# GLA recurrence and squared-ReLU layers on one Trainium2 core: fixed engine orders, two load queues, a finer first unit

## The chip, the cores and the metric

The kernel runs on one core of one Trainium2 chip. A core has a matrix engine (TensorE: PE, and PEld for its weight loads), VectorE (DVE), ScalarE (ACT), GpSimd (POOL) and SyncE (SP), each of which works through its own list of instructions in order, and 16 DMA engines. Here SP and POOL issue the DMAs: SP's on a queue that the profile calls q1 hardware_dynamic, POOL's on q0 software_dynamic. The metric is the device time of one execution in microseconds.

## The reference

```python
for t in range(S):                       # q, k, v, alpha: [4, 8, 768, 48], alpha in 0.8 to 1.0
    state = alpha[:, :, t, :, None] * state + einsum('bhd,bhe->bhde', k[:, :, t], v[:, :, t])
    y[:, :, t] = einsum('bhd,bhde->bhe', q[:, :, t], state)
x = y.transpose(0, 2, 1, 3).reshape(3072, 384)
out = square(maximum(x @ w_in, 0)) @ w_out      # w_in [384, 2048], w_out [2048, 384], all float32
```

A gated linear recurrence for 4 batches of 8 heads over 768 steps, and behind it two dense layers with a squared ReLU between them.

## The kernel before

**Units.** The 768 steps of a batch are cut in 3 stretches of T = 256 tokens; with 4 batches that makes G = 12 units, ordered stretch by stretch, so that units 0 to 3 are the first stretch of each batch. Two neighbouring tokens share a partition. Inside a unit the recurrence is computed as attention in two chunks: cumulated logarithms of alpha give decay factors, which multiply k and q; keys against queries give scores, a causal mask is laid over them, and scores times v plus queries times the carried state give x.

**Names.** Each operation has a name with its unit g, and the prediction uses them:

- `lda`, `ldk`, `ldq`, `ldv` load a unit's alpha, k, q, v (line 526; 1024 runs of 384 bytes, 384 KB), into one of 4 buffers;
- `ln` and `lm` take logarithms of alpha (lines 542, 604, 636, 675; from unit 2 on behind `pr`, a product of neighbours, line 633), `m1`, `m1i`, `m1s` sum them on TensorE (lines 548, 608, 642), `ei`, `ea`, `es`, `ec` are exponentials of the sums (563, 565, 621, 623, 653 and on), `bk`, `aq`, `lb` derive the other token's factors;
- `ekm` and `eqm` multiply k and q by the factors (578, 704, 709), `tr` transposes both (on TensorE for units 0 to 2, lines 590 and 732, with `et` bringing them back from PSUM, 597 and 739; by DMA on SP from unit 3 on, line 720), `vc` casts v (572, 699, 700);
- `p0` (and `p1` in unit 0) are the scores (898), `mk0` and `mk1` mask them (909), `kv` with `sa`, `sc`, `sd` forms the state (769, 864 to 875), `y` is the output of the attention (790, 801, 830, 837);
- `xe` takes x out of PSUM (929), `xt` transposes it (on TensorE, line 944, for units 0 to 3, by DMA on SP, line 950, from unit 4 on), `xv` brings it back (956, 958);
- `s1_g_u`, u = 0 to 7, is the first dense layer, 6 matmuls each (line 1000); `re` the ReLU out of PSUM (1008 on ScalarE, 1010 on VectorE), from two PSUM banks used by turns; `sq` the square (1018 VectorE, 1021 POOL, 1022 ScalarE); `s2_g_j_sg` the second layer, 4 matmuls each (1040); `oe` takes the result out (1047, 1049) and `out` stores it (1056).

In unit 0 the front works by halves of the heads, with an x = 0 or 1 in the name (`ln0_0`, `ln1_0`).

**What sets the order.** Every operation is entered with its reads and writes (`Program.add`, line 72). `Program.schedule` (line 117) plays the program through with a cost for each operation, priorities with hand-set offsets (`MOVED`, `CHOSEN`) and a model of the DMA queues; out of it come the engine of each operation and the order on each engine. `place` then puts the semaphore waits in, and each engine runs its list in order, so that a waiting instruction holds all behind it. `fill` (line 229) puts matmuls on zeros into TensorE's list wherever it would be idle before the first dense matmul; 34 of them here (line 1094).

**Loads and weights.** Units 1 and 2 load on POOL's queue, all others, the DMA transposes and all stores on SP's. The weights come in WS = 2 pieces each, cast to bfloat16 by the DMA, on POOL's queue. Loads are gated on the landing of others, and from unit 5 on on work of the unit before:

```python
AFTER = {1: (0, "a"), ("win", 0): (0, "k"), ("win", 1): (0, "k"), 2: ("win", 0), ("wout", 0): ("win", 1),
         ("wout", 1): (2, "k"), 3: ("wout", 0)}
AFTER.update({g: (g - 1, "q") for g in range(4, G)})
BEHIND = {"a": "ln", "k": "ekm", "q": "tr0_", "v": "tr0_"}     # of unit g - 1, for g >= 5
```

**The table load.** ScalarE's first operation, `table` (line 439), loads the set of function tables that has both logarithm and exponential. Nothing depends on it by name; its priority puts it first.

## Time and profile before

| what | value |
|---|---|
| timed runs | 175.56, 178.09, 178.64 us, median 178.09 |
| profiled execution, span | 178.0 us |
| PE busy | 168.6 us, 95% |
| DVE, ACT, POOL busy | 120.3, 119.4, 24.2 us |
| first dense matmul (L1000) | 18.21 us |
| HBM read, written | 25.17 MB, 4.72 MB |

The profiled execution is a run of its own; its time is its span, first to last instruction, 178.0 us. A line of a timeline gives start, length, engine, source line, operation, output and inputs, the count of merged instructions, and in brackets how long the engine had been idle before and what ended that. A line of a table of groups gives busy time and mean ns of one, then the idle time ahead of it. The matmuls' ends are modelled.

### The profile page before, as it was taken

Reading aid. Unit: us, or ns where it says so; the run is one execution under the profiler, and the core shown is the slowest. Engines: PE = TensorE matmul, PEld = TensorE weight load, DVE = VectorE, ACT = ScalarE, POOL = GpSimd, SP = SyncE. Lnnn points to the kernel's source line nnn. Section 1 sums busy time; section 2 is a strip of 40 time slices with the busy share of each in tenths; the row PEclk is TensorE's granted clock in tenths of the full one; section 3 lists DMA queues with packets and bytes.
Section 4 is the critical chain, followed back from the end, with each engine's and each line's share of the span. In section 5 each row is a group of like instructions: output and inputs, shape, how many; then the busy total and the mean of one; then the engine's idle time right before and its main releaser. Section 6 shows DMA issues by size and latency. Waiting matters only on the chain.

```text
span 178.0 us, 5087 instructions
## 1 busy us (share of the span) xinstructions
PE 168.6 (95%) x2232; PEld 130.6 (73%) x2234; DVE 120.3 (68%) x194; ACT 119.4 (67%) x214; POOL 24.2 (14%) x32
## 2 busy tenths in 40 slices
PE   7998998999996999999779999999999999999994
PEld 2655787856875778787558878878778787788773
DVE  5478579789885679984838876967958835423230
ACT  3838787867828588696388759859579554566450
POOL 3920951020304224200000000000000000000000
DMA  5999999979999799998999897999999692040022
GB/s 142 344 283 204 250 271 219 243 188 232 295 218 170 206 228 127 280 216 137 290 210 165 203 242 176 243 176 206 251 215 181 146 186 41 0 133 4 0 88 88
DMA packets 71030, 33.36 MB, mean 187 GB/s; under 512 B 67552, under 2 KB 67808, under 8 KB 71008
## 3 DMA queue, kind: packets, MB, share of 16 engines
q1 hardware_dynamic: 69024, 26.75, 67.6%
q0 software_dynamic: 1984, 6.29, 14.9%
q8 instruction: 17, 0.28, 0.6%
q14 instruction: 5, 0.04, 0.1%
HBM read 25.17 MB, written 4.72 MB: 168 GB/s over the span
## 4 chain that ended last, share of the span: by engine, by line
PE 74%; DMA 15%; ACT 5%; POOL 2%; DVE 1%; issue 1%; SPq 1%
PE psWH L1000 32%; PE psO L1040 29%; DMA raw<-in_v_dram 10%; DMA raw<-in_alpha_dram 5%; PE psZ L769 2%; PE psX L801 2%; POOL raw L526 2%; PE psX L898 2%; PE psX L790 2%; PE psX L970 1%; ACT rr L1008 1%; PE psZ L898 1%; PE psWH L642 1%; ACT vbf L700 1%; PE psZ L732 1%
## 5 line engine op out<-in xcount | busy, mean ns | idle before, releaser
L1000 PE MATMUL psWH<-xt,win 128*128 128x256 bf16 x576 | 73.9, 275 | 2.9 <-ACT rr L1008 1.8
L1000 PEld LDWEIGHTS psWH<-xt,win 128*128 128x128 bf16 x576 | 65.3, 145 | 8.1 <-ACT rr L1008 2.5
L1040 PE MATMUL psO<-wout,gt 128*128 128x384 bf16 x368 | 68.9, 326 | 1.9 <-ACT osb L1047 1.9
L1008 ACT ACTIVATE rr<-psWH 128x512 bf16<-128x512 f32 x85 | 50.1, 595 | 20.3 <-PE psWH L1000 18.6
L1040 PEld LDWEIGHTS psO<-wout,gt 128*128 128x128 bf16 x368 | 34.7, 98 | 20.5 <-ACT osb L1047 2.2
L1018 DVE TENSOR_TENSOR gt<-rr 128x1024 bf16<-128x1024 bf16 (+1 forms) x39 | 24.1, 622 | 25.3 <-ACT rr L1008 25.2
L909 DVE TENSOR_TENSOR pm<-psZ,caus 128x1024 bf16<-128x1024 f32 x12 | 14.6, 1219 | 2.4 <-PE psZ L898 2.4
L1022 ACT ACTIVATE gt<-rr 128x1024 bf16<-128x1024 bf16 (+1 forms) x18 | 15.2, 843 | 0.4
L909 DVE TENSOR_TENSOR pm<-psX,caus 128x1024 bf16<-128x1024 f32 x12 | 14.6, 1219 | 1.1 <-PE psZ L898 1.1
L929 ACT ACTIVATE xbf<-psX 128x768 bf16<-128x768 f32 x11 | 8.9, 809 | 7.1 <-PE psX L790 6.4
L700 ACT ACTIVATE vbf<-raw 128x768 bf16<-128x768 f32 x9 | 7.6, 841 | 8.6 <-DMA raw<-in_v_dram 8.6
L1047 ACT ACTIVATE osb<-psO 128x384 f32<-128x384 f32 x17 | 8.3, 489 | 5.2 <-PE psO L1040 4.8
L704 DVE TENSOR_TENSOR qks<-raw,eq 128x384 bf16<-128x384 f32 x18 | 9.8, 575 | 2.5 <-DMA raw<-in_q_dram 2.3
L1094 PE MATMUL psO<-zero 128*128 128x512 bf16 (+1 forms) x32 | 9.9, 437 | 1.5 <-DVE zero L447 1.3
L709 DVE TENSOR_TENSOR qks<-raw,ek 128x768 bf16<-128x768 f32 x11 | 10.5, 952 | 0.5 <-ACT ek L621 0.4
L1010 DVE TENSOR_SCALAR rr<-psWH 128x512 bf16<-128x512 f32 x11 | 7.6, 689 | 1.7 <-PE psWH L1000 1.2
L662 DVE TENSOR_TENSOR ek<-ek,raw 128x384 f32<-128x384 f32 x9 | 6.3, 705 | 1.4 <-ACT ek L653 1.4
L864 DVE TENSOR_TENSOR smd<-psZ,sbd 128x384 bf16<-128x384 f32 x8 | 4.4, 556 | 3.9 <-PE psX L790 3.9
L635 POOL TENSOR_TENSOR prd<-raw 128x384 f32<-128x384 f32 x4 | 4.0, 1002 | 19.5 <-DMA raw<-in_alpha_dram 19.5
L1094 PEld LDWEIGHTS psO<-zero 128*128 128x128 bf16 x34 | 3.2, 110 | 4.5 <-issue 1.9
L675 ACT ACTIVATE la<-raw 128x384 f32<-128x384 f32 x8 | 4.1, 518 | 3.4 <-DMA raw<-in_alpha_dram 3.2
L636 ACT ACTIVATE lab<-prd 128x384 bf16<-128x384 f32 x10 | 5.2, 521 | 1.7 <-DVE prd L633 1.7
(118 smaller groups left out, 171.7 us busy)
## 6 DMA issues: line engine op xcount, KB each, us to landing
out_dram<-osb SPq DMA_DIRECT2D x11, 384.0 KB, 4.1
raw<-in_alpha_dram SPq DMA_DIRECT2D x10, 384.0 KB, 3.6
raw<-in_k_dram SPq DMA_DIRECT2D x10, 384.0 KB, 5.3
raw<-in_q_dram SPq DMA_DIRECT2D x10, 384.0 KB, 3.9
raw<-in_v_dram SPq DMA_DIRECT2D x10, 384.0 KB, 5.2
win<-in_moe_w_in_dram POOLq DMA_DIRECT2D x2, 768.0 KB, 10.9
wout<-in_moe_w_out_dram POOLq DMA_DIRECT2D x2, 768.0 KB, 9.0
raw<-in_alpha_dram POOLq DMA_DIRECT2D x2, 384.0 KB, 4.6
```

The source lines that it names most:

```text
L700: name=f"vc{g}", alts={"act": (lambda e: e.activation(vout, vin, AF.Copy), act_ns(2 * HD))})
L704: add("dve", lambda e, j=j, dst=dst: e.tensor_tensor(dst, RAW[r][:, 2, :, j, :].rearrange("p (n x) d -> p n x d", x=2), EQ[la][:, j].rearr ...
L709: add("dve", lambda e, a=a, E=E: e.tensor_tensor(QKS[qs][:, a, :, :, 0:D], RAW[r][:, 1 + a].rearrange("p h j d -> p j h d"), E[la][:].rear ...
L909: add("dve", lambda e, hf=hf, psT=psT: e.tensor_tensor(PM[pm][:, hf].rearrange("p r n j t -> p (r n) (j t)"), psT[:, :, :].rearrange("p r ...
L929: add("act", lambda e: e.activation(XBF[x2][:], psX[:, :, 0:HD], AF.Copy), act_ns(2 * HD), p0 + 6100, reads=[("ps", "X", 0), ("ps", "X", 1 ...
L1000: ins = pe.matmul(psH[hb][:, i * T:(i + 1) * T], WIN[:, kk, hidden(fj)], mov, start=(kk == 0), stop=(kk == KT - 1))
L1008: add("act", lambda e, hb=hb, rr=rr: e.activation(rr, psH[hb], AF.Relu), act_ns(512), pu + 600, reads=[("ps", "H", hb)], writes=[("rr", rb ...
L1018: add("dve", lambda e, dst=dst, sq=sq: e.tensor_tensor(dst, sq, sq, ALU.mult), 148 + k * 267, pu + 1200, reads=[("rr", rb, h) for h in ran ...
L1022: "act": (lambda e, dst=dst, sq=sq: e.activation(dst, sq, AF.Square), act_ns(k * 512))})
L1040: ins = pe.matmul(psS, GT[gt][:, fj, j, :], WOUT[:, fj, :], start=(fj == 0), stop=(fj == FT - 1))
L1047: add("act", lambda e, j=j, psS=psS: e.activation(OSB[ob][:, j], psS, AF.Copy), act_ns(DM), ps_ + 700, reads=[keyS], writes=[("osb", ob, j ...
L1094: pr.fill(lambda n: lambda pe: pe.matmul(psO[:, 0:n], ZERO[:, 0:128], ZERO[:, 0:n], skip_group_check=True), ((512, 216, 420), (256, 109, 2 ...
```

## The change

It replaces the scheduler by five written-out lists, one for each engine, which name each operation once; an operation's engine is the list in which it stands. The fillers have a notation of their own in these lists ("~"), which the lists don't use. `place` and `emit` stay. Beside it:

- Loads from unit 1 on and stores may stand in SP's or POOL's list. Of the 49 load operations 29 stand in POOL's, and 6 of the stores. The gates on other loads go, but for two (alpha of unit 1 behind alpha of unit 0, the first piece of w_in behind k of unit 0), and so do those on the unit before.
- Unit 0's alpha is loaded in two halves; its state product is split in two steps (`kva0`, `kvb0`), its x is taken out, transposed and brought back in two halves (`xe0_0`, `xe1_0` and so on), and its second half's transposes use other PSUM banks.
- Each weight is loaded in three pieces, a quarter, a quarter and a half.
- ScalarE's `table` stands behind `xv0_0`, VectorE's fill of the zeros that the fillers used in the middle of its list.
- 55 ReLUs are ScalarE's and 41 VectorE's, and 20, 21 and 19 of the squares ScalarE's, VectorE's and POOL's.

```diff
-    HOP = 35
...
-    MOVED = {
...
-    CHOSEN = {
...
+    HALVED = {"qks": 3, "kqt": 3, "raw": 3, "ek": 3, "eq": 3, "acm": 2, "laf": 2, "xbf": 2, "xt": 2}
...
-    def schedule(self):
...
+    def schedule(self, tables, filler):
+
+        named = {o.name: o for o in self.ops}
+        queues = {}
+        for e, text in tables.items():
+            queues[e] = []
+            for word in text.split():
+                if word[0] == "~":
+                    after, n = filler[0], int(word[1:])
+                    o = Op({"pe": (filler[1](n), 0)}, 0, "fill")
+                    o.idx = len(self.ops)
+                    o.deps = {after: True}
+                    self.ops.append(o)
                 else:
...
+                    o = named.pop(word)
+                o.eng = e
+                o.fn, o.cost = o.alts[e]
+                o.pos = len(queues[e])
+                queues[e].append(o)
+        assert not named, sorted(named)
+        for o in self.ops:
+            if o.sem is not None:
+                key = o.sem[0] + o.eng
+                if key not in self.dma_sems:
+                    self.dma_sems[key] = self.nc.alloc_semaphore("d_" + key)
+                self.dma_count[key] = self.dma_count.get(key, 0) + 1
+                o.sem = (key, self.dma_count[key])
+        self.order = queues
+        at = dict.fromkeys(queues, 0)
+        free = dict.fromkeys(queues, 0)
+        left = len(self.ops)
+        while left:
+            before = left
+            for e, q in queues.items():
+                while at[e] < len(q) and all(d.end is not None for d in q[at[e]].deps):
+                    o = q[at[e]]
+                    o.start = max([free[e]] + [d.end for d in o.deps])
+                    free[e] = o.end = o.start + 1
+                    at[e] += 1
+                    left -= 1
+            assert left < before, [q[at[e]].name for e, q in queues.items() if at[e] < len(q)]
...
+TABLES = {
+    "pe": """
+        m10_0 tr00_0 m11_0 tr10_0 tr01_0 tr11_0 kva0 p1_0 p0_0 m11 y0 tr1_1 kvb0 xt1_0 xt0_0 tr0_1 s1_0_0 p0_1 m1i2
+        s1_0_1 kv1 s1_0_2 s1_0_3 y1 s1_0_4 s1_0_5 m1s2 xt1 s1_0_6 s1_0_7 tr0_2 s1_1_0 s1_1_1 m1i3 s1_1_2 s2_0_0_0
+        s1_1_3 s1_1_4 s2_0_0_1 tr1_2 s1_1_5 s1_1_6 m1s3 p0_2 s2_0_0_2 s2_0_0_3 s1_1_7 s2_0_1_0 s2_0_1_1 kv2 s2_0_1_2
...
+    "act": """
+        ln0_0 ei0_0 ea0_0 ln1_0 et00_0 ei1_0 ec0_0 ea1_0 ec1_0 et10_0 et11_0 et01_0 ln1 copycaus ei1 ea1 ec1 xe0_0
+        ln2 xv0_0 table ei2 re0_0 re0_1 sq0_1 ea2 re0_2 ec2 xe1 re0_4 re0_5 re0_6 re0_7 ln3 es2 et0_2 re1_1 ei3
+        re1_2 ea3 re1_4 sq0_7 ec3 re1_6 es3 oe0_0 vc2 sq1_6 vc3 oe0_1 xe2 ln4 ei4 ea4 re2_0 ec4 lm4 re2_3 es4 sq2_1
...
+    "dve": """
+        zlab0 zlinc zident zones zlstr zown zcaus1 zqks0 own0 own1 zcaus zlaf0 ekm0_0 eqm0_0 ekm1_0 eqm1_0 zlaf1
+        zqks1 mk1_0 mk0_0 sa0 eqm1 ekm1 xe1_0 zlab1 et1_1 xv1_0 et0_1 sc0 mk1_1 bk2 mk0_1 sa1 zqks2 re0_3 sq0_3 ekm2
+        xv1 sq0_5 re1_0 sc1 eqm2 re1_3 bk3 sq1_3 et1_2 sq1_1 re1_5 mk1_2 mk0_2 ekm3 sa2 sc2 pr4 sd2 eqm1_3 re1_7
+        eqm0_3 xv2 sa3 sc3 oe1_0 re2_1 eqm1_4 ekm4 re2_2 lb4 mk0_3 mk1_3 sq2_3 re2_5 eqm0_4 sa4 re2_6 pr7 sc4 xv3
+        lb5 eqm1_5 bk5 oe2_0 eqm0_5 re3_2 ekm5 mk0_4 mk1_4 re3_4 sq3_5 lb6 sa5 re3_7 sc5 ekm6 re3_6 zzero mk0_5
...
+    "pool": """
+        scaus1 sident slinc slstr lda1 ldq1 lda2 ldk1 scaus vc0 win0 win1 win2 pr2 ldk2 wout0 ldq2 vc1 wout1 wout2
+        sd0 ldv2 ldk3 pr3 aq2 sd1 sq0_6 aq3 sq1_5 ldq4 ldk4 sq1_7 sd3 bk4 ldq5 lda7 lda6 out0_1 vc4 ldv5 pr5 sq2_5
+        pr6 sd4 sq2_7 ldq6 ldk6 sq3_3 bk6 vc6 lda8 ldq7 out1_1 ldk7 ldv7 sq4_3 vc7 pr8 out2_1 ldq8 lda10 bk7 lda9
+        sq5_3 pr9 sq5_5 sq5_7 lda11 vc8 ldk9 pr11 sd7 bk10 ldk10 ldq10 ldv9 vc9 sq7_3 sq7_5 ldk11 out6_1 vc11 sq8_6
+        sq8_7 out7_1 sq9_3 sq9_6 sq10_3 sq11_1 sq11_5 out10_1
+    """,
...
+    "sp": """
+        lda00 ldk0 lda01 ldq0 ldv0 ldv1 lda3 ldv3 lda4 ldq3 ldv4 tr1_3 tr0_3 lda5 tr0_4 ldk5 tr1_4 ldv6 tr0_5 tr1_5
+        xt4 tr0_6 tr1_6 xt5 ldv8 ldq9 tr1_7 xt6 ldk8 tr0_7 out3_1 out4_1 tr0_8 tr1_8 xt7 tr1_9 tr0_9 ldq11 xt8 ldv11
+        ldv10 out5_1 tr0_10 tr1_10 xt9 tr0_11 tr1_11 xt10 xt11 out8_1 out9_1 out11_0 out11_10 out11_11
+    """,
+}
+
+
...
-    POOL_LOADS = {1: "akqv", 2: "akqv"}
+    HALF_LOADS = ((0, "a"),)
     RATIO = 4
     NRAW, NQKS, NKQT, NPM, NV, NXT, NGT, NRR, NOSB = 4, 3, 3, 2, 4, 4, 2, 4, 2
-    WS = 2
     LATE_STATE = (1, 2)
     ROW_TILED = tuple(range(PE_TRANSPOSED, G))
     BY_HEADS = (0,)
     IN_X = ()
     LAST_CUT = 272
     BY_TOKEN = (0, 1)
+    SPLIT_X = (0,)
+    SPLIT_KV = (0,)
+    WIDE = True
...
-    FS = FT // WS
+    PIECES = ((0, 4), (4, 4), (8, 8))
+
+    def piece(fj):
+        return max(w for w, (at, n) in enumerate(PIECES) if at <= fj)
 
     def hidden(fj):
 
-        w, e = divmod(fj, FS)
-        return slice(w * FS * 128 + e, (w + 1) * FS * 128, FS)
+        at, n = PIECES[piece(fj)]
+        return slice(at * 128 + fj - at, (at + n) * 128, n)
 
     def weight(lay, w):
-        cut = slice(w * FS * 128, (w + 1) * FS * 128) if lay == 0 else slice(w * FS, (w + 1) * FS)
+        at, n = PIECES[w]
+        cut = slice(at * 128, (at + n) * 128) if lay == 0 else slice(at, at + n)
         if lay == 0:
             src, dst = moe_w_in.rearrange("(kk p) n -> p kk n", p=128)[:, :, cut], WIN[:, :, cut]
         else:
-            src = moe_w_out[w * FS * 128:(w + 1) * FS * 128, :].rearrange("(p e) n -> p (e n)", e=FS)
+            src = moe_w_out[at * 128:(at + n) * 128, :].rearrange("(p e) n -> p (e n)", e=n)
             dst = WOUT[:, cut, :].rearrange("p e n -> p (e n)")
         key = ("win", "wout")[lay]
         load_op[key, w] = add("pool", lambda e: e.dma_start(dst, src), 930, W_PRIO[lay] + w, writes=[(key, w)], name=f"{key}{w}",
-                              dma=f"{key}{w}", lag=8600 / WS,
+                              dma=f"{key}{w}", lag=4300 / 8 * n,
...
-            dst, key = RAW[r][:, j], ("raw", r, j)
-            ring, cost, gate = "sp", 600, AFTER.get((g, nm), AFTER.get(g))
-            if nm in POOL_LOADS.get(g, ""):
-                ring, cost = "pool", 930
-            dst = dst.rearrange("p h j d -> p h (j d)")
-            load_op[g, nm] = add(ring, lambda e, dst=dst, src=src: e.dma_start(dst, src), cost, (L_PRIO[g] + j if ring == "sp" else W_PRIO[2] + 10 * g + j if g > 1 else -6e5 + j),
-                writes=[key], name=f"ld{nm}{g}", dma=f"{nm}{r}{ring}", lag=1230 if ring == "sp" else 1130,
-                after=([load_op[gate]] if gate else []) + ([named(f"{BEHIND[nm]}{g - 1}")] if g >= 5 else []))
+            dst, key = RAW[r][:, j].rearrange("p h j d -> p h (j d)"), ("raw", r, j)
+            gate = AFTER.get((g, nm))
+            parts = ((0, slice(0, 4)), (1, slice(4, 8))) if (g, nm) in HALF_LOADS else (("", slice(0, 8)),)
+            for x, hs in parts:
+                def run(e, dst=dst[:, hs], src=src[:, hs]):
+                    return e.dma_start(dst, src)
+
+                load_op[g, nm] = add("sp", run, 600, L_PRIO[g] + j, writes=[key if x == "" else key + (x,)],
+                                     name=f"ld{nm}{g}{x}", dma=f"{nm}{r}{x}", after=[load_op[gate]] if gate else [],
+                                     alts={"pool": (run, 930)} if g else {})
...
-                bank, psk = psZ[:, a, :].bitcast(BF16), [("ps", "Z", a)]
+                bank, psk = (psWH if x and WIDE else psZ)[:, a, :].bitcast(BF16), [(("ps", "W"), ("ps", "H", 0))[a] if x and WIDE else ("ps", "Z", a)]
...
+        if g in SPLIT_KV:
+            return (psH[1][:, 0:HD], psH[1][:, 0:HD]), [("ps", "H", 1), ("ps", "H", 1)]
...
-        if alone:
+        if g in SPLIT_KV:
+            run, cost, reads, writes = state_mm(g, (0,))
+            add("pe", run, 2 * cost, p0 + 2300, reads=reads, writes=writes, name="kva0", mode=("R", "R"))
+        elif alone:
...
+            run, cost, reads, writes = state_mm(g, (1,))
+            add("pe", run, 2 * cost, p0 + 2950, reads=reads, writes=writes, name="kvb0", mode=("R", "R"))
...
+        if g in SPLIT_X:
+            s = g % NXT
+            for c in range(2):
+                src, dst, key = psX[:, c, 0:HD], XBF[x2][:, c], [("ps", "X", c)]
+                add("act", lambda e, src=src, dst=dst: e.activation(dst, src, AF.Copy), act_ns(HD), p0 + 6100 + c,
+                    reads=key, writes=[("xbf", x2, c)], name=f"xe{c}_{g}",
+                    alts={"dve": (lambda e, src=src, dst=dst: e.tensor_copy(dst, src), dve_ns(HD))})
+            for c in range(2):
+                bank = psX[:, c, :].bitcast(BF16)[:, 0:HD]
+                key = [("ps", "X", c)]
+
+                def xtr(pe, c=c, bank=bank):
+                    for kk in range(KT):
+                        ins = pe.matmul(bank[:, kk * 128:kk * 128 + 128], XBF[x2][:, c, kk * 128:kk * 128 + 128], IDENT[:],
+                                        is_transpose=True)
+                    return ins
+
+                add("pe", xtr, pe_ns(3, 128), p0 + 6700 + c, reads=[("xbf", x2, c), ("ident",)], writes=key, name=f"xt{c}_{g}")
+                src = bank.rearrange("p (k j t) -> p k j t", k=KT, j=2)
+                dst = XT[s][:, :, :, c * 64:c * 64 + 64]
+                add("dve", lambda e, src=src, dst=dst: e.tensor_copy(dst, src), dve_ns(HD, 2), p0 + 7200 + c, reads=key,
+                    writes=[("xt", s, c)], name=f"xv{c}_{g}",
+                    alts={"act": (lambda e, src=src, dst=dst: e.activation(dst, src, AF.Copy), act_ns(HD))})
+            return
...
-                add("sp", lambda e, dst=dst: e.dma_start(dst, OSB[ob][:].rearrange("p j n -> p (j n)")), 600, ps_ + 1300,
-                    reads=[("osb", ob, 0), ("osb", ob, 1)], name=f"out{g}_1", dma=f"o{ob}", lag=1150)
+
+                def store(e, dst=dst):
+                    return e.dma_start(dst, OSB[ob][:].rearrange("p j n -> p (j n)"))
+
+                add("sp", store, 600, ps_ + 1300, reads=[("osb", ob, 0), ("osb", ob, 1)], name=f"out{g}_1",
+                    dma=f"o{ob}", alts={"pool": (store, 930)})
...
-    AFTER = {1: (0, "a"), ("win", 0): (0, "k"), ("win", 1): (0, "k"), 2: ("win", 0), ("wout", 0): ("win", 1),
-             ("wout", 1): (2, "k"), 3: ("wout", 0)}
-    AFTER.update({g: (g - 1, "q") for g in range(4, G)})
+    AFTER = {("win", 0): (0, "k"), (1, "a"): (0, "a")}
     load(0)
     load(1)
-    for w in range(WS):
+    for w in range(len(PIECES)):
         weight(0, w)
     load(2)
-    for w in range(WS):
+    for w in range(len(PIECES)):
         weight(1, w)
+    load(3)
...
-    pr.schedule()
-    pr.fill(lambda n: lambda pe: pe.matmul(psO[:, 0:n], ZERO[:, 0:128], ZERO[:, 0:n], skip_group_check=True),
-            ((512, 216, 420), (256, 109, 250)), min(o.start for o in pr.order["pe"] if o.name.startswith("s1_")), zero, 4600)
+    pr.schedule(TABLES, (zero, lambda n: lambda pe: pe.matmul(psO[:, 0:n], ZERO[:, 0:128], ZERO[:, 0:n], skip_group_check=True)))
```

More of the change, by code (lines that the diff above doesn't have):

```diff
@@ L1 @@
-import heapq
-import itertools
 import concourse.bass as bass
@@ L504, in hd @@
         return ap.rearrange("p (h d) -> p h d", h=H)
-    def named(x):
-        return next(o for o in pr.ops if o.name == x)
-    BEHIND = {"a": "ln", "k": "ekm", "q": "tr0_", "v": "tr0_"}
     def load(g):
@@ L766, in run @@
                 for j in range(2):
-                    for c in range(1 if last else 2):
+                    for c in chunks or range(1 if last else 2):
                         h0 = 64 * c
@@ L1004, in first_layer @@
             fjs = range(u * per, (u + 1) * per)
-            add("pe", s1, pe_ns(KT * per, T), pu, reads=[("xt", s)] + sorted({("win", f // FS) for f in fjs}),
+            add("pe", s1, pe_ns(KT * per, T), pu, reads=[("xt", s)] + sorted({("win", piece(f)) for f in fjs}),
                 writes=[("ps", "H", hb)], name=f"s1_{g}_{u}")
```

233 lines of the change are left out of this document (58 added, 175 removed), and 10 rows, old and new, of tables (CHOSEN, MOVED).

## The prediction

> **What bounds the kernel now.** I read the page first, then busy time by stage, then TensorE's waits, and last the timelines of the engines that end those waits.
>
> ```profile
> span 178.0 us, 5087 instructions
> ...
> PE 168.6 (95%) x2232; PEld 130.6 (73%) x2234; DVE 120.3 (68%) x194; ACT 119.4 (67%) x214; POOL 24.2 (14%) x32
> ...
> GB/s 142 344 283 204 250 271 219 243 188 232 295 218 170 206 228 127 280 216 137 290 210 165 203 242 176 243 176 206 251 215 181 146 186 41 0 133 4 0 88 88
> ...
> q1 hardware_dynamic: 69024, 26.75, 67.6%
> q0 software_dynamic: 1984, 6.29, 14.9%
> ```
>
> TensorE is busy 95% of the span, so the 5% and the time before its real work begin are all that an order of work can win. The span (178.0) is the median of the timed runs (178.09) within 0.1, so sums against it need no correction. Stages, cut at the first dense matmul of unit 0, that of unit 1, the end of the visible waits, and the last matmul:
>
> ```profile
> 18.20:27.50 9.30, 8.38 (x147) 7.35 (x147) 6.45 (x10) 7.54 (x14) 6.82 (x9) 1.00 1.03 259
> 27.50:90.00 62.50, 58.66 (x820) 45.83 (x821) 50.44 (x74) 43.78 (x83) 10.17 (x9) 1.00 0.97 219
> 90.00:175.50 85.50, 85.43 (x1080) 68.37 (x1080) 51.08 (x79) 57.04 (x98) 0.00 (x0) 1.00 0.70 148
> ```
>
> The columns are stretch, length, then PE, PEld, DVE, ACT, POOL busy. From 90 on PE is never idle (85.43 of 85.50): nothing can be won there, only lost. From 27.5 to 90 it idles 62.50 - 58.66 = 3.84. TensorE's own waits name who ends them:
>
> ```profile
> PE psO L1040 <- ACT osb L1047: 1.9, 1, 1.9
> PE psWH L1000 <- ACT rr L1008: 1.8, 2, 1.6
> ```
>
> ScalarE is named twice, but it was itself held, each time just before PE's gap, by an input that had not landed and stood ahead of the work PE needed:
>
> ```profile
> 53.94 0.52 ACT L675 ACTIVATE la<-raw 128x384 f32<-128x384 f32 x1 [2.57 <-DMA raw<-in_alpha_dram]
> 88.65 0.84 ACT L700 ACTIVATE vbf<-raw 128x768 bf16<-128x768 f32 x1 [2.58 <-DMA raw<-in_v_dram]
> ```
>
> So the bound is TensorE, plus loads that arrive late up to 90, plus 18.21 us before the first dense matmul, a chain that runs from alpha of unit 0 to it (its first and last piece: start, length, what):
>
> ```profile
> 0.80 3.49 DMA raw<-in_alpha_dram
> ...
> 18.21 1.53 PE psWH L1000 x12
> ```
>
> **The change, part by part.** First the start, since each microsecond there shifts everything behind it. These are the prices on ScalarE and VectorE:
>
> ```profile
> 0.80 1.28 ACT L441 ACT_TABLE_LOAD   x1 [0.80 <-PEq L1111]
> 2.98 0.42 ACT L476 ACTIVATE caus<-caus 64x256 bf16<-64x256 bf16 x1 [0.89 <-POOL caus L450]
> 4.38 0.94 ACT L542 ACTIVATE laf<-raw 128x384 bf16<-128x384 f32 x2 [0.99 <-DMA raw<-in_alpha_dram]
> 6.04 0.49 ACT L563 ACTIVATE ek<-psX 128x384 f32<-128x384 f32 x1 [0.72 <-PE psX L554]
> 7.85 0.31 ACT L567 ACTIVATE acm<-psX 128x4 f32<-128x4 f32 x2
> 8.06 1.08 ACT L599 ACTIVATE kqt<-psZ 128x512 bf16<-128x512 bf16 x2
> 9.77 0.83 ACT L604 ACTIVATE laf<-raw 128x768 bf16<-128x768 f32 x1
> ```
>
> ```profile
> 9.63 0.42 DVE L597 COPY kqt<-psZ 128x512 bf16<-128x512 bf16 x1 [0.61 <-PE psZ L590]
> 9.99 1.23 DVE L909 TENSOR_TENSOR pm<-psX,caus 128x1024 bf16<-128x1024 f32 x1
> 11.46 0.55 DVE L867 TENSOR_TENSOR smd<-psWH,own 128x384 bf16<-128x384 f32 x1
> 15.24 0.96 DVE L709 TENSOR_TENSOR qks<-raw,ek 128x768 bf16<-128x768 f32 x1 [0.43 <-ACT ek L621]
> 16.98 1.51 DVE L739 COPY kqt<-psZ 128x1024 bf16<-128x1024 bf16 x2
> ```
>
> **Order of the start: +1.2.** Half of alpha lands earlier by half of 393 KB at 344 GB/s (second slice of the page), 0.57: at 3.7. From the start of ln0_0 to ei0_0 took 6.04 - 4.38 = 1.66, so ei0_0 is at 5.4. ScalarE's new queue then holds, up to copycaus, four exponentials (1.96), the second half's logarithm (0.47), two acm (0.31), three evictions (1.62), unit 1's logarithm (0.83) and copycaus itself (0.42): 5.6, and some 1.4 of round trips over TensorE and VectorE between them: 12.4. Before, copycaus was at 2.98. Both masks need it and now begin behind it: mk1_0 and mk0_0 2.46, sa0 0.55, then eqm1 and ekm1 (1.91) ahead of xe1_0 (0.55): 17.9. et1_1 (0.75) and xv1_0 (0.42) follow: 19.1; with tr0_1, which stands ahead of s1_0_0, 19.4. That is 1.2 behind 18.21. The split halves of x shorten each step by about 0.25 to 0.4; they pay only if the chain reaches them earlier, and it doesn't. Bounds: -1.9 (below) and +2.
>
> **Table loads: +4.0.** The explicit load, free at 0.80 while ScalarE waits for alpha, moves behind xv0_0. Ahead of it now stand ln0_0, ei0_0, ln1_0, ei1_0, ln1, ei1, ln2: logarithm and exponential by turns. The builder of the program has to put a load wherever an activation finds its function missing. I take it that for a logarithm it picks a table without the exponential, and the other way round: seven loads of 1.28 ahead of the explicit one, all but the first on a running queue. Hidden are the first, most of the one beside m10_0 (1.28 against the 1.1 from 4.38 + 0.94/2 to 6.04; with the hand-over 0.3 shows) and those of ei1 and ln2, beside 2.46 of masks and 1.91 of products. In the open are those of ln1_0 (1.28), ei1_0 (1.1, partly beside m11_0) and ln1 (1.28): 4.0. The bounds are 0 (one load serves all) and 7 x 1.28 = 9.0 (nothing hides). The first dense matmul is then at 18.2 + 1.2 + 4.0 = 23.4.
>
> [...]
>
> **Fillers gone: +0.9.** The new TensorE queue has no filler matmuls.
>
> ```profile
> 1.25 4.02 PE L1094 MATMUL psO<-zero 128*128 128x512 bf16 x9 [1.25 <-DVE zero L447]
> ...
> 6.60 0.81 PE L1094 MATMUL psO<-zero 128*128 128x512 bf16 x3
> ```
>
> Nine took 4.02 (447 ns each) at the beginning, three took 0.81 (270 ns) after 6.6: TensorE starts at about half rate. Without fillers that phase falls on the dense work behind 23.4. Four microseconds at half rate lose 2.0; the 18.2 to 27.5 stage is paced in part by ScalarE (7.54 busy of 9.30) and covers the rest. I take 0.9, bounds 0 and 2.
>
> **Loads, stores and weights shared out: -3.8.** Gates of one load on another's landing, and of unit g's loads on unit g-1's front, go; the rows with 2.57 and 2.58 are their result. A start 5.2 later gives every load that much more time as well. I count the whole 3.84 as won; bounds 0 and 3.84 plus the 0.92 of the stage before. What hangs on POOL's queue instead:
>
> ```profile
> L526 POOL DMA_DIRECT2D raw<-in_alpha_dram x2 | 2.0, 996 | 9.8 <-DMA win<-in_moe_w_in_dram 8.2 <-DMA raw<-in_alpha_dram 1.6
> L635 POOL TENSOR_TENSOR prd<-raw 128x384 f32<-128x384 f32 x4 | 4.0, 1002 | 19.5 <-DMA raw<-in_alpha_dram 19.5
> L1021 POOL TENSOR_TENSOR gt<-rr 128x512 bf16<-128x512 bf16 (+1 forms) x3 | 4.0, 1323 | 4.9 <-ACT rr L1008 3.2 <-DVE rr L1010 1.7
> ```
>
> POOL issues 41 transfers instead of 12: 29 more at 0.9 to 1.0, some 27; it also takes 19 squares instead of 3, at 1.3 some 21 more. With the old 24.2 that is 72 of 178, off the path. The third pieces of both weights are in that count; transfers in flight hide their issue.
>
> ```profile
> L1008 ACT ACTIVATE rr<-psWH 128x512 bf16<-128x512 f32 x85 | 50.1, 595 | 20.3 <-PE psWH L1000 18.6
> L1010 DVE TENSOR_SCALAR rr<-psWH 128x512 bf16<-128x512 f32 x11 | 7.6, 689 | 1.7 <-PE psWH L1000 1.2
> ```
>
> ScalarE's relus fall from 85 to 55, VectorE's rise from 11 to 41 at 0.69: 21 more, against 18 squares fewer of about 0.6. VectorE stays near 130 of 178, under TensorE. In-order queues add waits: vc1 on POOL waits for v of unit 1 on SP, with wout1, wout2, sd0 and unit 2's v behind it (s2_0_0_0 needs wout0 alone, which is ahead); on SP the transposes of unit 3 stand behind ldv4, which waits for vc0. Covered by transfers already queued, I price these at 0; uncovered, they cost what the third rival does.
>
> **Sum: 178.0 + 1.2 + 4.0 + 0.9 - 3.8 = 180.3.**
>
> **The rivals.** *One table load serves all.* Then the 4.0 falls away: 176.3. For it: the program before shows one load only; against it, that one was explicit and first. [...] 0.18.
>
> *The start follows the smaller first weight piece.* If the round trips are shorter than I add up and the loads hide, s1_0_0 waits for a quarter of w_in alone. POOL's next load was gated on the first half's landing, and a quarter of w_in is 1.65 of that queue's time (26.5 us, 14.9% of the span, for 6.29 MB; 0.39 MB):
>
> ```profile
> 17.98 0.90 POOL L526 DMA_DIRECT2D raw<-in_alpha_dram  x1 [8.16 <-DMA win<-in_moe_w_in_dram]
> ```
>
> A quarter is there at about 17.98 - 1.65 = 16.3. Then -1.9 replaces +5.2: 173.2. Against it: copycaus behind ln1. 0.17.
>
> *SP's early loads starve: slower.* Alpha of unit 3 goes on SP at once, without a gate, while POOL's queue is never empty. A packet on q0 lasts 0.149 x 178.0 x 16 / 1984 = 0.214, on q1 0.676 x 178.0 x 16 / 69024 = 0.028. If an engine serves the queues packet by packet, SP gets 0.028 / 0.242 = 12% of it. POOL's part until then, eight loads and all weights, is as much as the whole q0 row: 124 packets an engine, 0.149 x 178.0 = 26.5 us, from about 8 on (half of alpha at 5.4, then 3.49 - 1.14 from issue to data). Unit 1's v and unit 3's alpha on SP are two loads of 1024 runs of 384 bytes, 128 packets an engine: lda3 lands at 8 + 26.5 + 124 x 0.028 = 38. POOL's pr3 (1.0) waits for it, behind pr3 aq2 and sq0_6; then ScalarE's ln3 (0.5), behind it all its relus; then m1i3, which the new TensorE queue has ahead of s1_1_2. TensorE is there at 23.4 + 9.3 + 0.9 + 1.5 = 35.1 and goes on at 39.7: 4.6 more, 184.9. It decides once lda3 lands after 33.5. For it: unequal packets; against it: no stretch of the trace has both queues full for long. [...] 0.20.
>
> *The sharing brings nothing:* both queues use the same 16 engines, and the waits stay: 180.3 + 3.8 = 184.1. Against it: after 90 the same loads cost TensorE nothing. 0.07.
>
> **How the numbers follow.** The forecast has 0.38, with 180.3. Two per cent (174.5 to 181.7) is about what a measurement of this kernel can tell from no change. Faster: the early start, 0.17, and 0.05 of the single load with its bound of 0.92. Slower: starving and no gain, 0.26 of their 0.27, and 0.08 of the forecast where more loads lie open (up to 5.0 more, 185.3). The same: the rest, 0.44. The range 172.5 to 186 takes in these cases and the bound of the table loads.
>
> **What would show it.** In the changed profile: eight ACT_TABLE_LOAD rows or one; the first L1000 matmul at 23 (19 or 16 by the rivals); its first dozen at half rate; no wait of ScalarE for alpha or v over 0.5 between 40 and 90; PE busy throughout from there. I am wrong if the first dense matmul is before 18, if a POOL row L635 waits for alpha at 30 to 38, or if PE idles after 90, because a relu stands behind masks on VectorE.

## The result, and the profile after

| | before | after |
|---|---|---|
| median of the timed runs | 178.37 us | 196.53 us |
| runs | 175.56 to 178.75 | 193.13 to 198.22 |
| ratio, 95% interval | | 1.101, 1.0747 to 1.1274 |
| span of the profiled execution | 178.0 us | 195.6 us |
| first dense matmul (start of its weight load) | 18.21 us | 24.41 us |

The change makes the kernel 10% slower; 180.3 was forecast. Single executions of either kernel run longer at a lower granted clock (after 197.29 at 0.974 beside 193.13 at 0.991, before 180.1 at 0.99 beside 176.93 at 1.0 in a later round); the ratios leave them out, and where a kernel had only one undisturbed execution, its lowest time stands here instead of a ratio.

The page of the changed kernel (the slices are 40 equal parts of the span, in tenths):

```profile
span 195.6 us, 5041 instructions
...
PE 167.4 (86%) x2200; PEld 130.4 (67%) x2200; DVE 130.7 (67%) x198; ACT 104.1 (53%) x185; POOL 90.8 (46%) x95
...
PE   0365899999999998059999799869999999999995
...
PEclk9999999999999999657999999999999999999999
...
q1 hardware_dynamic: 46336, 16.13, 40.6%
q0 software_dynamic: 5360, 16.91, 31.8%
```

TensorE falls from 95% to 86%, nearly all in three places: a start with little work (the fillers, which had counted as work, are gone), a hole at slices 16 and 17 (counted from 0), and a dent at 25 and 26. POOL's queue now moves half the bytes, in 5360 packets against SP's 46336. The same in stages (stretch, length, then PE, PEld, DVE, ACT, POOL busy, granted clock, DMA share, GB/s):

```profile
0.00:24.40 24.40, 11.81 (x154) 8.99 (x154) 10.33 (x27) 18.73 (x28) 13.73 (x24) 1.00 1.03 249
24.40:34.40 10.00, 9.35 (x159) 7.93 (x158) 8.22 (x12) 7.55 (x13) 3.68 (x4) 1.00 1.08 255
34.40:77.50 43.10, 42.70 (x618) 32.87 (x614) 39.68 (x55) 27.66 (x54) 32.00 (x31) 1.00 0.81 200
77.50:92.50 15.00, 7.16 (x51) 4.83 (x41) 4.73 (x8) 4.36 (x8) 0.00 (x0) 0.66 0.53 104
92.50:130.00 37.50, 33.22 (x488) 25.82 (x488) 33.40 (x48) 20.36 (x40) 22.79 (x21) 1.00 0.96 208
```

From 34.4 to 77.5 TensorE idles 0.40 in all: there the shared queues do what was forecast. Then it stops for 7.8 us, in a stage whose granted clock is 0.66. Its waits and its timeline say for what:

```profile
PE psWH L963 <- DMA xt<-xbf: 10.4, 2, 7.8
PE psX L478 <- ACT laf L472: 6.6, 2, 5.4
...
PE psWH L963 <- DVE rr L973: 1.2, 1, 1.2
```

```profile
85.51 0.83 PE L963 MATMUL psWH<-xt,win 128*128 128x256 bf16 x3 [7.84 <-DMA xt<-xbf]
```

The DMA transpose of x of unit 4 (`xt4`, on SP) was issued at 74.35. POOL had just put five transfers on its queue:

```profile
72.85 0.93 POOL L454 DMA_DIRECT2D raw<-in_alpha_dram  x1
73.78 0.88 POOL L454 DMA_DIRECT2D raw<-in_q_dram  x1
74.65 0.57 POOL L1021 DMA_DIRECT2D out_dram<-osb  x1
75.21 0.89 POOL L454 DMA_DIRECT2D raw<-in_k_dram  x1
76.09 0.88 POOL L454 DMA_DIRECT2D raw<-in_v_dram  x1
```

The DMA view from 76 to 85.5 (queue: packets, MB, share of the 16 engines; then the transfers with their us from issue to landing):

```profile
q0 software_dynamic: 461, 1.74, 86.5%
q1 hardware_dynamic: 800, 0.20, 12.2%
...
raw<-in_v_dram POOLq DMA_DIRECT2D x1, 384.0 KB, 10.2
xt<-xbf SPq DMA_TRANSPOSE x1, 11.1
```

SP's queue has 12.2% of the engines' time, and a transpose that landed in 3.3 before takes 11.1. Its 800 packets are the transpose, 0.20 MB. `xt7` meets three loads of POOL's in the same way (idle 2.6, the second of the two waits). Where both queues are full, at the start, one moves as many packets as the other. The DMA views from 20 to 24 and from 28 to 32:

```profile
q0 software_dynamic: 378, 0.71, 93.4%
q1 hardware_dynamic: 377, 0.14, 20.3%
...
q0 software_dynamic: 283, 0.93, 95.0%
q1 hardware_dynamic: 282, 0.10, 12.6%
```

One packet against one packet, 378 to 377 and 283 to 282, but POOL's packets carry five to nine times as much. In the hole itself it is 800 to 461, so it is not one against one throughout; that POOL's transfers hold the transpose up is shown below by moving them, the rule by which the engines divide their time is not.

The other part is the start. ScalarE's groups of table loads (count, busy, mean ns, idle before):

```profile
L472 ACT ACT_TABLE_LOAD x2 | 2.6, 1283 | 3.6 <-DMA raw<-in_alpha_dram 3.5
L493 ACT ACT_TABLE_LOAD x2 | 2.6, 1283 | 0.0
L534 ACT ACT_TABLE_LOAD x1 | 1.3, 1283 | 0.0
L551 ACT ACT_TABLE_LOAD x1 | 1.3, 1283 | 0.0
L566 ACT ACT_TABLE_LOAD x1 | 1.3, 1283 | 0.0
L368 ACT ACT_TABLE_LOAD x1 | 1.3, 1283 | 0.0
```

Eight loads instead of one, as forecast. The first starts only when alpha of unit 0 has landed; the others stand between two activations, nearly without a gap (ScalarE's timeline):

```profile
3.54 1.28 ACT L472 ACT_TABLE_LOAD   x1 [3.54 <-DMA raw<-in_alpha_dram]
4.83 0.52 ACT L472 ACTIVATE laf<-raw 128x384 bf16<-128x384 f32 x1
5.38 1.28 ACT L493 ACT_TABLE_LOAD   x1
6.67 0.49 ACT L493 ACTIVATE ek<-psX 128x384 f32<-128x384 f32 x1
```

### The profile page after: what moved, and what is told of

It reads as the page before. It is cut to its first block, busy times and chain, and to the rows that moved or that the text cites. A ratio compares the mean times of both kernels' runs of the same rounds, so it can differ in the third digit from the quotient of the medians.

```text
span 195.6 us, 5041 instructions
## 1 busy us (share of the span) xinstructions
PE 167.4 (86%) x2200; PEld 130.4 (67%) x2200; DVE 130.7 (67%) x198; ACT 104.1 (53%) x185; POOL 90.8 (46%) x95
## 3 DMA queue, kind: packets, MB, share of 16 engines
q0 software_dynamic: 5360, 16.91, 31.8%
## 4 chain that ended last, share of the span: by engine, by line
PE 59%; DVE 15%; DMA 13%; ACT 6%; POOL 3%; issue 2%; SPq 1%; DVEq 0%; ACTq 0%
PE psWH L963 24%; PE psO L1003 22%; DMA xt<-xbf 9%; DVE pm L847 4%; DMA kqt<-qks 3%; DVE gt L981 3%; POOL gt L984 2%; DVE rr L973 2%; DVE qks L634 1%; PE psX L733 1%; PE psZ L701 1%; PE psZ L662 1%; DVE xbf L894 1%; DMA raw<-in_alpha_dram 1%; PE psX L933 1%
## 5 line engine op out<-in xcount | busy, mean ns | idle before, releaser
L984 POOL TENSOR_TENSOR gt<-rr 128x1024 bf16<-128x1024 bf16 (+1 forms) x19 | 32.0, 1686 | 63.9 <-DVE rr L973 43.5
L971 ACT ACTIVATE rr<-psWH 128x512 bf16<-128x512 f32 x55 | 32.5, 597 | 43.7 <-PE psWH L963 43.4
L973 DVE TENSOR_SCALAR rr<-psWH 128x512 bf16<-128x512 f32 x41 | 27.9, 685 | 29.1 <-PE psWH L963 28.8
L985 ACT ACTIVATE gt<-rr 128x512 bf16<-128x512 bf16 (+1 forms) x20 | 16.3, 820 | 2.5 <-DVE rr L973 2.4
L981 DVE TENSOR_TENSOR gt<-rr 128x1024 bf16<-128x1024 bf16 (+1 forms) x21 | 15.8, 752 | 1.8 <-ACT rr L971 1.4
L629 POOL CAST vbf<-raw 128x768 bf16<-128x768 f32 x7 | 6.4, 921 | 5.6 <-DMA raw<-in_v_dram 5.6
L454 POOL DMA_DIRECT2D raw<-in_alpha_dram x8 | 7.4, 921 | 3.1 <-DMA raw<-in_alpha_dram 3.1
L454 POOL DMA_DIRECT2D raw<-in_k_dram x9 | 8.1, 903 | 0.0
L811 POOL TENSOR_TENSOR sbd<-tmp,acm 128x384 bf16<-128x384 f32 x5 | 4.2, 831 | 7.7 <-DVE tmp L809 7.7
L454 POOL DMA_DIRECT2D raw<-in_q_dram x8 | 7.3, 908 | 0.0
```

The lines of the kernel that those rows point to most:

```text
L454: return e.dma_start(dst, src)
L971: add("act", lambda e, hb=hb, rr=rr: e.activation(rr, psH[hb], AF.Relu), act_ns(512), pu + 600, reads=[("ps", "H", hb)], writes=[("rr", rb ...
L973: alts={"dve": (lambda e, hb=hb, rr=rr: e.tensor_scalar(rr, psH[hb], 0.0, None, ALU.max), dve_ns(512))})
L981: add("dve", lambda e, dst=dst, sq=sq: e.tensor_tensor(dst, sq, sq, ALU.mult), 148 + k * 267, pu + 1200, reads=[("rr", rb, h) for h in ran ...
L984: alts={"pool": (lambda e, dst=dst, sq=sq: e.tensor_tensor(dst, sq, sq, ALU.mult), 200 + k * 840), "act": (lambda e, dst=dst, sq=sq: e.act ...
L985: "act": (lambda e, dst=dst, sq=sq: e.activation(dst, sq, AF.Square), act_ns(k * 512))})
```

## The experiments

All times are medians; the kernel before was run beside them each time and had 176.93 to 178.5. A diff of a list shows a stretch as it was (-) and as it became (+); "..." stands for words left out, and where only + is shown, the words named there stand in that order.

**One part undone at a time.** `a_table` puts the table load first, `a_five` moves the five transfers to SP behind the transpose:

```diff
 "act": -ln0_0 ei0_0 ... ln2 xv0_0 table ei2      +table ln0_0 ei0_0 ... ln2 xv0_0 ei2
 "pool": -vc6 lda8 ldq7 out1_1 ldk7 ldv7 sq4_3    +vc6 sq4_3
 "sp":   -xt4 tr0_6                               +xt4 lda8 ldq7 out1_1 ldk7 ldv7 tr0_6
```

> The changed kernel with one edit: ScalarE's table load stands first in its list again. Theory 1 (the start is held by the extra table loads): one table load instead of eight, the first dense matmul at about 20.4 instead of 24.4 us, and the time about 4 us shorter, 191 to 192. Theory 2 (the time is set later, by the wait of TensorE for the transpose xt4): the start comes 4 us earlier, but the wait at 77 us takes the gain back, and the time stays within 1.5 us of 196.

> The changed kernel with one edit: the five transfers that POOL issues beside the transpose xt4 (alpha, q, k, v of units 7 and 8 and the store of unit 1) stand on SP's list right behind xt4. Theory 1 (packets of POOL's queue hold the transposes on SP's): xt4 lands in 3 to 4 us instead of 11, TensorE's wait of 8 us at 77 goes, and with it the slow clock behind it: 185 to 188. Theory 2 (xt4 is slow because DMA is busy whatever the queue, or the wait only moves to the next transpose): no more than 3 us won, 193 or more.

`a_table`: 195.01 (lowest 191.04). The first dense matmul comes at 20.83 instead of 24.41, and TensorE leaves the hole at 82.19 instead of 85.51; the hole itself stays (`xt4` 11.2 to land). Of the 3.6 that the start wins the time shows 1.5 by the medians, 2.1 by the lowest: theory 2 is the nearer one. `a_five`: 188.92, ratio 1.0652 (1.0581 to 1.0723). `xt4` lands after 3.3 and the hole is gone; `xt7` still takes 6.1. That is theory 1's mechanism, with a time 0.9 above its range.

**All later loads and stores on SP** (from q of unit 4 on, in the order in which they had been issued), without and with the table load first:

```diff
 "pool": -ldq4 ldk4 ldq5 lda7 lda6 out0_1 ... ldk11 out6_1 out7_1 out10_1
 "sp":   +(the same, in between)
```

> The changed kernel with all loads and stores from q of unit 4 on taken off POOL's list and merged into SP's in the order in which they were issued. Theory 1 (two queues taking turns is what slows the transposes): all transposes xt land within 5 us, no wait of TensorE for one over 1.5 us, 182 to 186. Theory 2 (SP's issue time is what the second queue relieved): SP is late with loads and transposes, waits of ScalarE and VectorE for loads appear, and the time is 190 or more.

> Both edits, the table load first and one queue. If the two causes are separate and add up: 4 us below the one-queue kernel, 178 to 182. If the start is hidden behind the loads: no more than 1 us below the one-queue kernel.

`a_onequeue` 189.02, 1.0633 (1.0572 to 1.0693); `a_table_onequeue` 186.57, 1.050 (1.044 to 1.056). The holes are gone here too (TensorE's longest wait for a transpose of x is 2.0 and 2.3), but 9 us stay. Both times lie between the ranges of their theories: the table load is worth 2.4 here, neither 4 nor under 1.

**The transfers that meet a transpose, and nothing else.** `g_eight` moves, beside the five, ldk10, ldq10 and ldv9 to SP behind `xt7`; `f_min` also puts the table load first.

```diff
 "pool": -bk10 ldk10 ldq10 ldv9 vc9       +bk10 vc9
 "sp":   -xt7 tr1_9                       +xt7 ldk10 ldq10 ldv9 tr1_9
```

> The changed kernel with the table load first, and with the eight transfers that stood beside two of the transposes of x moved from GpSimd's queue to SP's: the five behind xt4 and ldk10, ldq10, ldv9 behind xt7. All other loads and stores stay shared out. Theory (of the sharing only the meeting with the transposes costs): both transposes land within 5 of their issue and the time is 183 to 185, below the 186.57 of the kernel with all later transfers on SP. Rival (two queues cost also where no transpose is held up): 186 to 189.

> The changed kernel with only the eight transfers moved from GpSimd's queue to SP's (behind xt4 and xt7), the table load left where the change put it. Theory (the extra table loads delay the first dense matmul by 3.5 to 4 and nothing behind it gives that back): 184 to 185.5, 3 to 4.5 above f_min (180.91). Rival (late loads and transposes take up most of a later start): 181 to 183.

`g_eight` 184.53, 1.0456 (1.0368 to 1.0545); `f_min` 180.91, 1.023 (1.0154 to 1.0305). Both theories hold; `f_min` is even below its theory's 183. It is 2.7 points of the ratio below the kernel with one queue and the table load first: outside the two meetings, sharing the transfers out is worth having in this kernel. `f_min` in the stage that has the hole, and its `xt4`:

```profile
31.00:90.00 59.00, 58.04 (x814) 44.92 (x812) 55.02 (x76) 36.81 (x74) 36.05 (x34) 1.00 0.93 225
```

```profile
DMA to landing us min/median/max: 3.1/3.1/3.1
```

**The meeting in the kernel before.** `b_three_pool` sends three of its loads through POOL, behind pr6 and without their gates, while SP transposes:

```diff
+pr.move("ldq6", "pr6", "sp", "pool", ("ldq5", "tr0_5"))
+pr.move("ldv6", "ldq6", "sp", "pool", ("ldq5", "tr0_5"))
+pr.move("lda7", "ldv6", "sp", "pool", ("ldq6", "ln6"))
```

> The kernel before with one thing changed: three loads (q and v of unit 6, alpha of unit 7) taken off SP's queue and put on GpSimd's behind pr6, without their gates, so that they are in flight when SP issues the DMA transpose of x of unit 4. Theory (while GpSimd's queue is full SP's queue advances packet against packet, and a transpose of x is many small ones): that transpose lands 6 to 10 us behind its issue instead of 3.25, TensorE waits 2 to 6 us for it between 70 and 78, and the time is 180 to 184. Rival (the long transpose of the changed kernel came from something else in its order): it lands within 5 us and the time stays within 1 of before.

182.24 (lowest 179.43). The views of this kernel from 61 to 67 for the transposes of k and q of unit 5 (4.0 to 6.3 before), from 64 to 80 for `xt4` (3.3 before), and TensorE's timeline:

```profile
DMA to landing us min/median/max: 6.0/7.3/8.5
...
DMA to landing us min/median/max: 7.6/7.6/7.6
...
72.66 0.64 PE L939 MATMUL psX<-kqt 64*64 64x128 bf16 x16 [4.12 <-issue]
```

`xt4` is as slow as the theory said, but TensorE's stop is another one than forecast: 4.1, ahead of the scores of unit 5. The profile names no releaser for it; the second of the two transposes of k and q, issued at 64.07 and 8.5 on its way, is there at 72.6, when it ends. So transposes beside POOL's loads are slow also in a kernel that has neither the new lists nor the table loads. What that costs is less certain: the lowest time, 179.43, is below the range.

**The late loads of the kernel before.** `d_nogates` takes the gates off its loads from unit 4 on; `b_act_order` leaves them and moves the two waiting operations of ScalarE behind TensorE's work:

```diff
+    for op in pr.order["sp"]:
+        if op.name[:2] == "ld" and int(op.name[3:]) > 3:
+            g = int(op.name[3:]) - 1
+            gates = [f"ldq{g}", f"ln{g}", f"ekm{g}", f"tr0_{g}"]
+            for d in [d for d in op.deps if d.name in gates]:
+                del op.deps[d]
```

```diff
+pr.move("lm5", "oe1_1", "act")
+pr.move("vc7", "sq5_1", "act")
```

> The kernel before without the gates on its loads from unit 4 on (neither on the landing of the unit before's q nor on its logarithm, product or transposes); all on SP, in the same order. Theory (the loads were late because the DMA engines were full, 0.97 of them busy between 27.5 and 90, not because of the gates): 0 gained, 176 to 179, the DMA share between 27.5 and 90 still 0.95 or more. Rival (the step of the prediction, by which the gates make the loads late): the two waits of 2.57 and 2.58 shrink below 1 and the time falls by 1.5 to 3.8, 173 to 175.5.

> The kernel before with two operations of ScalarE moved behind work that TensorE waits for: lm5 (waits for alpha of unit 5) behind re2_4 and oe1_1, and vc7 (waits for v of unit 7) behind oe4_0, re5_0, re5_1 and sq5_1. Nothing else is changed. Theory (the two waits of 2.57 and 2.58 us cost TensorE its two longest stops, 1.9 and 1.6, only by standing first): 174.5 to 176. Rival (TensorE stops at the next late load instead): 177 to 178.5.

`d_nogates`: 175.31, 0.9933 (0.9887 to 0.998), the only interval that lies below the kernel before. Here the rival, the prediction's own reading, was right on the two waits (ScalarE's timeline):

```profile
52.92 0.53 ACT L716 ACTIVATE la<-raw 128x384 f32<-128x384 f32 x1 [0.32 <-DMA raw<-in_alpha_dram]
...
86.09 0.85 ACT L741 ACTIVATE vbf<-raw 128x768 bf16<-128x768 f32 x1 [0.33 <-DMA raw<-in_v_dram]
```

They fall from 2.57 and 2.58 to 0.3, though the DMA engines are as full as before (share 1.02 from 27.5 to 90, 0.97 before). But the gain is 1.2 (0.4 to 2.0), not 3.84, and TensorE still idles 1.82 in that stage. `b_act_order`: 177.06, 1.0041 (0.9987 to 1.0095): nothing. The two stops of TensorE are gone from its profile, and one of 0.9 (for another logarithm) is new.

**The start and the rest.** `c_fill` and `g_fill` put fillers (8 of 512 columns and, by the lists, 24 of 256, on zeros) into `a_table_onequeue` and `f_min`.

```diff
 "pe":  +~512 (6) m10_0 +~512 ~512 tr00_0 m11_0 +~256 tr10_0 +~256 tr01_0 ... y0 +~256 ~256
 "dve": +zzero (first)
```

> The changed kernel with the table load first and the later loads and stores on SP (186.57 with these two alone, first dense matmul 21.56), and in addition filler matmuls on zeros in TensorE's list wherever it idled before its first dense matmul (8 of 512 columns and 25 of 256), with the zeros filled first on VectorE. Theory: without fillers TensorE does its own first work cold (y of unit 0 took 1.15 us against 0.76 in the kernel before); that is worth 0.4 to 1.0 before the first dense matmul and about 1 behind it, so 184.5 to 185.5. Rival: the stage behind is paced by ScalarE and VectorE, and the fillers change less than 0.5: 186 to 187.

> f_min (180.91) with the filler matmuls of c_fill. Theory (a cold TensorE costs 1 to 2, as y of unit 0 at 1.15 against 0.76 shows): 179 to 180. Rival (the first stage is paced by other engines, as c_fill's 0.4 said): 180.4 to 181.2.

186.18 beside 186.57, 181.09 beside 180.91: nothing that can be measured, as the rivals said. Yet y of unit 0, from its first start to its last end, went from 1.28 to 0.87 and 0.86, and the first dense matmul from 21.56 to 19.92 and from 20.84 to 20.50: an earlier start need not reach the end. `c_fill_start` and `g_fill_start` add a mended start, the second with the first piece of w_in behind lda1; `h_best` also puts two relus of unit 8 ahead of a late product:

```diff
 "act": +table copycaus          "pool": +scaus1 scaus
 "dve": +sa0 xe1_0 xv1_0 eqm1 ekm1     "pe": +xt0_0 s1_0_0 tr1_1 tr0_1
 "pool": +lda1 win0 ldq1          "dve": +eqm1_10 re8_2 re8_3 ekm11
```

> As c_fill, and the start's order mended: the copy of the mask right behind the table load on ScalarE, its second half made earlier on GpSimd, x of unit 0 taken out and brought back ahead of unit 1's products on VectorE, and unit 1's transposes behind the first dense group on TensorE. Theory (the order of the start costs what it delays): the first dense matmul comes at 18 to 19 instead of 21 and the end moves by most of it: 182 to 183.5. Rival (what is won at the start is given back at the next load or transpose, as with the table load, where 1.5 of 3.6 arrived): 184 to 186.

> g_fill with the start mended as in c_fill_start, and the first piece of w_in moved in GpSimd's queue from behind unit 1's q and k and unit 2's alpha to right behind unit 1's alpha (in c_fill_start the first dense matmul waited 3.0 for that piece). Theory (the order of the start costs what it delays): the first dense matmul at 17 to 18 and the time 177 to 179. Rival (unit 1's loads, now later, hold its attention up and take it back): 179.5 to 181.5.

> g_fill_start, and two relus of unit 8 moved ahead of the product that waits for k of unit 11 on VectorE; f_min's TensorE stood 1.86 for them at 130. Theory: the stop is gone, 1 to 2 below g_fill_start. Rival (the next late load stops TensorE instead): within 0.5 of g_fill_start.

`c_fill_start` 190.02 (lowest 185.03); `g_fill_start` 184.5, 1.0454; `h_best` 184.2, 1.0437. The theory fell: on `f_min` the mended start is slower (184.5 beside `g_fill`'s 181.09, and the intervals do not meet). `c_fill_start` tells nothing: its median is above `c_fill`'s, its lowest time below. In `g_fill_start` x of unit 0 comes back on ScalarE behind a logarithm, which waits for POOL's product, which waits for alpha of unit 2, now later in the queue (timelines of TensorE, ScalarE and POOL):

```profile
20.16 1.33 PE L963 MATMUL psWH<-xt,win 128*128 128x256 bf16 x6 [3.06 <-ACT xt L889]
...
19.20 0.53 ACT L566 ACTIVATE lab<-prd 128x384 bf16<-128x384 f32 x1 [2.78 <-POOL prd L565]
...
18.18 0.99 POOL L565 TENSOR_TENSOR prd<-raw 128x384 f32<-128x384 f32 x1 [5.56 <-DMA raw<-in_alpha_dram]
```

So the first dense matmul comes at 20.16, not at 17 to 18, and the second group, for which unit 1's transposes now stand behind the first, at 24.83 instead of `g_fill`'s 22.13.

`i_copy` therefore mends the copy of the mask alone, on `f_min`, and `i_copy_re8` adds the two relus:

```diff
 "act": +table copycaus          "pool": +scaus1 scaus
 "dve": +eqm1_10 re8_2 re8_3 ekm11     (i_copy_re8)
```

> f_min (180.91, first dense matmul 20.84) with one thing more: the copy of the mask right behind the table load on ScalarE instead of behind unit 1's logarithm, and its second half made first on GpSimd. Theory (both masks and all behind them wait for that copy, 3.2 us of VectorE's idle time in f_min): the first dense matmul at 19.6 to 20.2 and the time 179.5 to 180.5. Rival (the first piece of w_in or the return of x stands next): the first dense matmul not before 20.5, 180.6 to 181.5.

> i_copy with the two relus of unit 8 ahead of the product that waits for k of unit 11 on VectorE. Theory: the stop of 1.86 at 130 goes and nothing takes its place: 1.5 to 2 below i_copy, 177.5 to 179, which is within 1 per cent of before. Rival (something else is late there): within 0.7 of i_copy.

181.99, 1.0123 (1.0012 to 1.0233), and 180.4, 1.0186 (1.0121 to 1.0251): neither told apart from `f_min`. The first dense matmul stays at 21.22 and 20.54 (20.84 in `f_min`); the copy is not what it waits for. VectorE's timeline of `i_copy_re8` shows what is:

```profile
12.28 1.23 DVE L845 TENSOR_TENSOR pm<-psZ,caus 128x1024 bf16<-128x1024 f32 x1 [2.12 <-PE psZ L834]
...
16.16 1.20 DVE L637 TENSOR_TENSOR qks<-raw,eq 128x768 bf16<-128x768 f32 x1 [1.07 <-ACT eq L551]
17.29 0.95 DVE L637 TENSOR_TENSOR qks<-raw,ek 128x768 bf16<-128x768 f32 x1
18.16 0.54 DVE L871 CAST xbf<-psX 128x384 bf16<-128x384 f32 x1
```

The masks begin a microsecond earlier, but the half of x (L871) stands behind unit 1's products, and these wait for unit 1's exponential.

**The squares on POOL.** `e_sq_act` gives them to ScalarE, `e_sq_re_act` also 19 of VectorE's relus, with `xt4` ahead of lda8 and ldq7:

```diff
 "pool": -sq0_6 sq1_5 sq1_7 ... sq11_5     "act": +(the same, each where its inputs are ready)
 "dve":  -re1_5 re2_1 ... re11_5           "act": +(the same)      (e_sq_re_act)
```

> c_fill (186.18) with GpSimd's 19 squares on ScalarE, each put where its inputs are ready. Theory (GpSimd's squares hold VectorE's two-input operations up, a product of 0.95 took 2.40 beside one, and ScalarE has room, 94 of 184 busy): VectorE's products are back at 0.95 to 1.0 and the time falls by 1 to 3, 183 to 185. Rival (the long products are hidden by other waits): 185.5 to 187.

> e_sq_act, and in addition 19 of VectorE's 41 relus on ScalarE, where the kernel before has most of them, and the transpose of x of unit 4 one transfer earlier in SP's queue. Theory (with the kernel before's division of the relus the masks and the relus no longer stand behind each other on VectorE, and the transpose comes 1.3 earlier): 1 to 3 below e_sq_act, 180.5 to 183.5. Rival (the division is not what holds TensorE up, or ScalarE becomes the bound): within 1 of e_sq_act or slower.

`e_sq_act` 188.63 (lowest 184.31): not told apart from `c_fill`. `e_sq_re_act` 184.41, 1.0463 (1.0375 to 1.055), 1.3% below `c_fill`, with intervals that overlap. The products (11 each) in `c_fill` and in `e_sq_act`:

```profile
L639 DVE TENSOR_TENSOR qks<-raw,ek 128x768 bf16<-128x768 f32 x11 | 14.1, 1283 | 3.1 <-DMA raw<-in_k_dram 3.1
```

```profile
L639 DVE TENSOR_TENSOR qks<-raw,ek 128x768 bf16<-128x768 f32 x11 | 11.1, 1008 | 1.9 <-DMA raw<-in_k_dram 1.8
```

So POOL's squares do slow them, from 1008 ns to 1283; that this costs time is not shown.

## Why the prediction was wrong

By the ratios, on 178: after, +18.0; `a_five` +11.6, `g_eight` +8.1, `f_min` +4.1. Each kernel holds the one before it, so five transfers cost 6.4, three more 3.5, the table loads 4.0, and 4.1 stay. By the intervals the first share is uncertain by 4.9 either way, the others by 2.0, 2.1 and 1.3; and the shares hold for this order of undoing, for with the hole in place the table loads are worth only 1.5 to 2.1 (`a_table`).

- **Loads, stores and weights shared out: -3.8. This step failed,** in the sentence that the waits of the new queues, "covered by transfers already queued", are priced at 0. Eight transfers cost 9.9. It looked for waits between loads on in-order lists; it did not ask which of SP's own transfers, the transposes of x that TensorE waits for with nothing behind them, would share the engines with POOL's long packets (in the hole 1.74 MB in 461 packets, the transpose 0.20 MB in 800). The gain was mis-sized as well: in the kernel before, the gates from unit 4 on are worth 1.2. Sharing did take the idle time away where no transpose was held up (0.96 from 31 to 90 in `f_min`), but the 3.84 came from one execution and not from the typical one: the profiled executions with both figures have a time 1.7 above their span (after 195.6 and 197.29), so the span of 178.0 would be that of a run of about 179.7, and "need no correction" was wrong.
- **The rival "SP's early loads starve"** had the mechanism and its share, 12%: from 28 to 32, packet against packet (283 to 282), SP's queue has 12.6%. (The 12.2% in the hole agrees by luck, since the packets are 800 to 461 there.) It had the wrong place: alpha of unit 3 landed at 11.95, early: from 7 to 9 the engines moved 1722 packets, all of SP's queue; alpha of unit 4 took 24 and nobody waited for it. The price was paid at 77, by a transpose. 184.9 was too low for that reason.
- **Table loads: +4.0.** Right in number and size: eight loads, and 4.0 by the ratios of `g_eight` and `f_min` (3.6 by medians). Which of them lie in the open it had wrong twice, and the two errors cancel, which is luck. The first load was to be hidden, but it waits for alpha (the row of 3.54), and the first logarithm starts at 4.83 instead of `f_min`'s 3.38, 1.45 later. The one of ln1 was to cost 1.28, but adds 0.1: the delay is 3.87 at ei1_0 (11.30, 7.43) and 3.95 at ln1 (16.00, 12.05). The first dense matmul was forecast at 23.4 and came at 24.41. The rival with one load for all fell: the profile has eight. Around a load nothing more is seen lost: the one at 5.38 has its 1.28, and the exponential behind it starts at 6.67.
- **Order of the start: +1.2.** Mis-sized: 2.6 (first dense matmul of `f_min` at 20.84, with one table load). The step had the sequence of VectorE right. Its masks were to begin at 12.4 and begin at 13.23 in `f_min`; it also left out that the first of the two products waits for unit 1's exponential, so that an earlier copy of the mask, on which it laid the weight, wins nothing measurable (`i_copy`).
- **Fillers gone: +0.9.** Mis-sized: 0 within the uncertainty, in two pairs; it was inside the bounds of 0 and 2.
- **"PE idles after 90, because a relu stands behind masks on VectorE"** came about in kind: in `f_min` two relus stand behind a product that waits 2.48 for k of unit 11, and TensorE stops for 1.9:

```profile
129.81 0.96 DVE L637 TENSOR_TENSOR qks<-raw,ek 128x768 bf16<-128x768 f32 x1 [2.48 <-DMA raw<-in_k_dram]
```

With 2.6 of the start this makes 4.5 against the 4.1 that stay; yet taking the stop away (`h_best`, `i_copy_re8`) did not measurably pay, so how the last 4.1 divide stays open.

## What to carry to other kernels

When transfers move to a second queue, look first at what stays on the first one and is waited for at once: here eight bulk transfers beside two transposes cost more than all else. Where both queues were full at the start, they shared packet for packet and not byte for byte (378 to 377 packets, 0.71 to 0.14 MB), so put the urgent, small-packet transfer where no bulk transfer is in flight, or queue the bulk behind it, as `f_min` does (`xt4` lands in 3.1 instead of 11.1). And do not count a wait of one profiled execution as won: of 3.84 the gates brought 1.2.
